# Attention rows kept in two tiles of four heads each, with stores of their own; gate weights loaded two steps earlier; the first q unit loaded from ScalarE's queue

## The chip, the cores and the metric

The kernel runs on one core of one Trainium2 chip. The metric is device time of one execution in microseconds, the median of several runs. The five instruction queues of the core that matter here are TensorE (PE, with its weight loads PEld), VectorE (DVE), ScalarE (ACT), GpSimd (POOL) and SyncE (SP); nearly all DMAs of this kernel are issued by SP, one after the other in the order of its queue.

## The reference

A linear attention feeds a mixture of experts. Cut to what matters:

```python
# q, k, v: (8 batches, 8 heads, 576 rows, 64), w_phi (64, 128), float32
def phi(x):
    p = einsum('bhsd,df->bhsf', x, w_phi)
    p = p - max(abs(p), axis=-1, keepdims=True)
    return concatenate([exp(p), exp(-p)], axis=-1)         # 256 features
kv  = einsum('bhsf,bhsd->bhfd', phi(k), v);  z = sum(phi(k), axis=2)
att = einsum('bhsf,bhfd->bhsd', phi(q), kv) / (einsum('bhsf,bhf->bhs', phi(q), z)[..., None] + 1e-6)
x   = att.transpose(0, 2, 1, 3).reshape(4608, 512)        # one row per token, 8 heads side by side
out = x.copy()
rows with x @ w_skip > 0 choose e = argmax(x @ w_gate), g = its softmax weight:
    out = x + g * (maximum(x @ w1[e], 0) @ w2[e])           # 8 experts, 512 -> 1024 -> 512
```

## The kernel before

The program has an attention part (to about 385 us) and an expert part after it.

**Units and steps.** The attention works on units of one batch and four heads: unit n is batch n // 2, heads 0 to 3 if n is even ("first half", `hq` 0) and 4 to 7 if odd ("second half", `hq` 1). There are 16 units for k and 16 for q, called k0 to k15 and q0 to q15 below. A loop over steps `t` takes half a unit (one pair of heads) of k and of q per step, q two steps behind k, so that unit n of k and unit n - 1 of q both enter at step 2n. In a step DVE transposes the loaded tile (`xT<-raw`, L316), PE projects it (`ps_A`, L327), DVE takes the maximum and subtracts it (L337, L338), ACT takes the exponentials (L352, L369), PE sums over k (`ps_K`, L408), ACT copies that to `kva` (L415), POOL copies a part of it to `kvs` (L420), PE turns that (`ps_V`, L360) and multiplies q (`ps_O`, L473), ACT copies the result to `os` (L477), and POOL divides it by its denominator into the row tile `xm` (L456) and the logits tile `lgm` (L458). The orders of PE, DVE, ACT and POOL are written out by hand from step 3 to step 35; SP's order is set by a scheduler, which puts a DMA where its own estimate has it ready.

**Loads.** `st_load` brings a unit of k or q with 8 DMAs of 32 x 18 x 32 elements (`raw<-in_k_dram`, `raw<-in_q_dram`, L283), `st_loadv` a unit of v with 4 larger ones (`v<-in_v_dram`, L292) and 4 small ones (`vt<-in_v_dram`, L299). There are four `raw` buffers, so k and q are loaded about one unit ahead. `setup_aug` loads the weights of the gate and of the skip score (`wgs`, L137 and L138), which POOL copies into `wgd` (L142) for the logits; it is called in step 3.

**Row tiles and stores.** Each batch has one tile `xm` of 128 x 4 x 514: 512 columns for eight heads, then the gate weight and the row's number. The last 64 rows of two batches share a tile `xt`. The first half's four heads are stored to `xrows` (a table in memory from which the experts gather their rows) when its two pairs are done: `store_half`, L493, and L495 for `xt`, columns 0 to 255. The second half's columns, with gate and number, follow later (`store_rows`, L591 and L593), and the function `rest` writes all 512 columns of a batch to the output (L671, 4 DMAs; L676, 4 for `xt` in odd batches). POOL writes the second half's heads into the same tile `xm` out of which the first half's store reads. Although these are other columns, the program makes the write wait for the store, as the order of POOL further down shows.

**Expert part.** After the counts of batch 5, `pick` chooses experts; SP loads weight chunks of 512 KB (`wraw_c<-in_moe_w_dram`, L188 and L191), ACT and POOL or DVE split them (L199, L204) and PE multiplies. The first experts' loads stand in SP's queue among the last stores of the attention.

Of the kernel before, what the change touches and what calls it, by code (L numbers as in the profile page):

```python
# [8 lines left out]
F32 = mybir.dt.float32  # L9
# [3 lines left out]
AF = mybir.ActivationFunctionType  # L13
# [4 lines left out]

P = 128
SLOT = 256  # L20
CFG = {'late': 1, 'gp': (0, 1, 2, 4, 6, 8, 9, 11, 12, 14, 17, 19, 21), 'rows': 9.0, 'tab': (2, 4, 5, 6, 6, 7, 8, 9, 10, 11, 12, 13, 16, 20, 32), 'ql': 0, 'cp': 0, 'seq': ('E', 'E', 'E', 'C', 'C', 'SC', 'C', 'DS', 'C', 'D'), 'post': (2, 4, 1), 'man': (3, 36), 'eng': ('PE', 'DVE', 'Activation', 'Pool'), 'nb': {'K': 1, 'O': 1, 'A': 2, 'P': 3, 'U': 2}, 'apools': (('ld', 2), ('hl', 4), ('up', 5), ('zp', 2), ('ep', 7), ('kvp', 5), ('ac', 1), ('xp', 3)), 'mpools': (('rawp', 1), ('mx', 2), ('wseta', 1), ('mo', 2), ('wsetb', 1), ('wsetc', 1), ('rawq', 1)), 'lag': (2, 2, 3, 0), 'order': ('Lv12KQebRcdBuExzwl', 'L01aKQ2ebRcdBuExwzy'), 'vl': 0, 'at': 3, 'eb': (2, 2), 'ub': 4, 'stage': (1, 1, 2, 2), 'dve': ('0', '1n', '2k', 'qt'), 'pd': 1}


@with_exitstack
def kernel(
# [20 lines left out]
    NQ = H // 4  # L46
# [8 lines left out]
    XW = DM + 2  # L55
# [19 lines left out]
    ac = pools["ac"]  # L75
# [155 lines left out]
    with actx:  # L231
# [26 lines left out]
        kva_of = {}  # L258
        kva_last = [None]
        xt_of = {}  # L260
        xm_of = {}
        et_of = {}
        kvt_of = {}
        kvs_of = {}
# [8 lines left out]
                c.pop(0)()  # L273
                last = c

        def st_load(u):
            src = kv_in[u.kind]
            u.raw = ld.tile([P, 2, 18, 32], F32, tag="raw", name="raw", bufs=4)
            for pr in range(2):
                for hd in range(2):  # L280
                    for dh in range(2):
                        r = (2 * hd + dh) * 32
                        nc.sync.dma_start(  # L283
                            out=u.raw[r:r + 32, pr],
                            in_=src[u.g, pr][hd * 32:hd * 32 + 32, :, dh * 32:dh * 32 + 32],
                        )

        def st_loadv(u):
            u.v0 = ld.tile([P, 4, 4 * D], F32, tag="v", name="v")
            u.vt = vts[u.g % len(vts)]  # L290
            for q4 in range(4):
                nc.sync.dma_start(  # L292
                    out=u.v0[q4 * 32:q4 * 32 + 32].rearrange("p h (t c) -> p h t c", c=D),
                    in_=vv[u.g][:, :, 4 * q4:4 * q4 + 4, :],
                )
            for pr in range(2):
                for q2 in range(2):
                    r = pr * 64 + q2 * 32
                    nc.sync.dma_start(out=u.vt[r:r + 32, pr, :, 0:D], in_=vv[u.g][:, 2 * pr:2 * pr + 2, 16 + q2, :])  # L299

        def st_v(u):
            u.v = vms[u.g % len(vms)]
# [159 lines left out]
        def st_use_q(u, pr, th):  # L462
            if th == 0:
                u.os = xp.tile([P, 8, NAUG], F32, tag="os", name="os", bufs=2)
            kva = kva_of[u.g]
            ov = bank("O")[:, 0:4 * NAUG].rearrange("p (t c) -> p t c", c=NAUG)
            e = u.e[pr]
            h0 = u.hq * 4 + 2 * pr
            for j in range(2):
                for hd in range(2):  # L470
                    for half in range(2):
                        for s in range(2):
                            nc.tensor.matmul(  # L473
                                ov[s * 64:s * 64 + 64, 2 * j + hd, :], e[:, half, s, 4 * hd + 2 * th + j],
                                kva[:, half, 2 * pr + hd, :], start=(half == 0), stop=(half == 1),
                            )
            nc.scalar.activation(out=u.os[:, 4 * th:4 * th + 4], in_=ov, func=AF.Copy)  # L477
            if th == 0:
                return
            if u.hq == 0 and pr == 0:  # L480
                xm_of[u.b] = (
                    xp.tile([P, 4, XW], F32, tag="xm", name="xm"),
                    xp.tile([P, 4, H, E + 1], F32, tag="lgm", name="lgm"),
                )
            xm, lgm = xm_of[u.b]

            def finish():
                c = slice(0, 4 * D)
                if pr == 0:
                    return  # L490
                if u.hq == 0:
                    def store_half(b=u.b, xm=xm):
                        nc.sync.dma_start(out=rowm[b][:, :, c], in_=xm[:, :, c])  # L493
                        if b % 2 == 1:
                            nc.sync.dma_start(out=rowt[b // 2][:, c], in_=xt_of[b // 2][0][:, 0, c])  # L495
                    later.append((now[0] + 1, store_half, "R"))
                else:
                    later.append((now[0] + CFG["pd"], lambda: post(u.b), "R"))

            norms.append(norm(u.os, 8, xm[:, :, h0 * D:(h0 + 2) * D].rearrange("p a (h d) -> p a h d", d=D),  # L500
                              lgm[:, :, h0:h0 + 2, :], 4) + [finish])

        def st_use_qt(u):

            if u.b % 2 == 0:
# [12 lines left out]
            nc.scalar.activation(out=os, in_=ov, func=AF.Copy)
            if u.hq == 0:
                xt_of[u.b // 2] = (  # L520
                    xp.tile([P, 1, XW], F32, tag="xt", name="xt"),
                    xp.tile([P, 1, H, E + 1], F32, tag="lgt", name="lgt"),
                )
            xt, lgt = xt_of[u.b // 2]
            norms.append(norm(os, 4, xt[:, :, u.hq * 4 * D:(u.hq + 1) * 4 * D].rearrange("p a (h d) -> p a h d", d=D),
                              lgt[:, :, u.hq * 4:(u.hq + 1) * 4, :], 1))

        def sm(tag, shape, dt=F32, bufs=2):
# [1 line left out]

        def post(b):
            last = b == B - 1
            xm, lgm = xm_of[b]
            t0 = 9 * (b // 2) + 4 * (b % 2)
            parts = [(xm, lgm, 0, 4)]
            if b % 2 == 1:
                xt, lgt = xt_of[b // 2]
                parts.append((xt, lgt, 4, 1))
            nt = 4 if b % 2 == 0 else 5
            T = slice(t0, t0 + nt)  # L540
# [42 lines left out]
            def gates():  # L583
                for xx, lg, o, n in parts:
                    nc.scalar.activation(
                        out=xx[:, :, DM + 1:XW], in_=sid[:, t0 + o:t0 + o + n].rearrange("p (t o) -> p t o", o=1), func=AF.Copy)
                    nc.vector.reciprocal(out=xx[:, :, DM:DM + 1], in_=gt[:, o:o + n].rearrange("p (t o) -> p t o", o=1))

            def store_rows():
                c = slice(4 * D, XW)  # L590
                nc.sync.dma_start(out=rowm[b][:, :, c], in_=xm[:, :, c])  # L591
                if b % 2 == 1:
                    nc.sync.dma_start(out=rowt[b // 2][:, c], in_=xt[:, 0, c])  # L593

            if last:
                best()
                exps()
                hot()
                gates()
                store_rows()  # L600
            else:
                best()
                for dt, f in zip(CFG["stage"], (exps, hot, gates, store_rows)):
                    later.append((now[0] + dt, f, "R"))
            S = 4
            nsh = S * E
# [59 lines left out]
                later.append((now[0], add, "R"))  # L666

            def rest():
                for q4 in range(4):
                    rr = slice(q4 * 32, q4 * 32 + 32)  # L670
                    nc.sync.dma_start(out=outv[b][:, q4 * 4:q4 * 4 + 4, :], in_=xm[rr, :, 0:DM])  # L671
                if b % 2 == 1:
                    for par in range(2):
                        for q2 in range(2):
                            rr = slice(par * 64 + q2 * 32, par * 64 + q2 * 32 + 32)
                            nc.sync.dma_start(out=outv[b - 1 + par][:, 16 + q2, :], in_=xt[rr, 0, 0:DM])  # L676

            if last:
                rests.extend((rank, rest))
# [45 lines left out]
        later = []  # L725
# [15 lines left out]
        for t in range(NPR + F + LQ + 2):  # L741
# [7 lines left out]
                setup_aug()  # L749

            if t == CFG["ql"]:
                st_load(units["q"][0])
            u = unit("k", t + CFG["vl"])
            if u:
                st_loadv(u)
# [626 lines left out]
```

## Time and profile before

| | us |
|---|---|
| median of 3 runs | 653.09 (650.76 to 654.57) |
| the profiled execution, its own time | 649.49 |
| its span, first to last instruction | 647.8 |
| PE busy in it | 542.2 (84%) |
| DVE busy | 445.8 (69%) |
| ACT busy | 340.3 (53%) |
| POOL busy | 304.4 (47%) |
| SP's queue moved by DMA | 97.61 MB, 58.1% of 16 DMA engines' span |

All later numbers are of the profiled execution, whose own time lies 1.7 us over its span and 3.6 us under the median of the runs. In the views, a row of the timeline gives start, duration, engine, line, operation, tiles, count, and in brackets the idle time before it with what ended it. A row of waits gives who waited for whom: total, times, longest. SP has no busy share in the page, since issuing a DMA is not counted as work; its rows in the timeline show how long each issue held the queue.

### The profile page before, as it was taken

The page shows a single profiled execution, that of the slowest core. Times are in us where ns is not written, and L with a number is a line of the kernel's source. Part 1 is how long each engine was busy: PE and PEld are TensorE (multiplying, and loading weights), DVE is VectorE, ACT ScalarE, POOL GpSimd, SP SyncE. Part 2 cuts the span into 40 slices and gives each one's busy share as a digit, 9 for nine tenths or more (in the row PEclk, how much of TensorE's full clock was granted, in tenths as well). Part 3 has the DMA queues.
Part 4 walks back from the last instruction along what each step waited for, and adds up shares of the span by engine and source line. Part 5 has one row for each costly group of instructions (what it writes and reads, how often), then busy time and mean ns, then how long its engine had stood idle before and what let it go on. Part 6 is the DMA issues. An engine that isn't in the chain of part 4 may idle for free. (4 is left out here: it accounts for less than half of the span.)

```text
span 647.8 us, 20883 instructions
## 1 busy us (share of the span) xinstructions
PE 542.2 (84%) x8638; PEld 502.0 (77%) x8638; DVE 445.8 (69%) x787; ACT 340.3 (53%) x561; POOL 304.4 (47%) x497
## 2 busy tenths in 40 slices
PE   2648977979969698798798679779999988999994
PEld 2648977879869698798797677659888978898893
DVE  5528865858947678478586376994887788856751
ACT  2136755645747367466665533433466755774630
POOL 2012314524434335234354974797466958469121
PEclk9869997989979989799899899798999999999998
DMA  6665567566675675766623768668758787687500
GB/s 111 113 106 118 97 126 151 111 169 126 111 202 111 131 171 106 199 109 129 149 76 79 260 185 288 210 220 253 231 180 269 239 296 251 232 278 261 199 18 28
DMA packets 223746, 108.47 MB, mean 167 GB/s; under 512 B 162339, under 2 KB 204451, under 8 KB 223650
## 3 DMA queue, kind: packets, MB, share of 16 engines
q1 hardware_dynamic: 220320, 97.61, 58.1%
q0 software_dynamic: 3200, 9.45, 4.2%
q8 instruction: 69, 1.13, 0.7%
q14 instruction: 27, 0.22, 0.1%
q10 hardware_dynamic: 130, 0.07, 0.0%
HBM read 83.86 MB, written 24.02 MB: 167 GB/s over the span
## 5 line engine op out<-in xcount | busy, mean ns | idle before, releaser
L204 POOL TENSOR_TENSOR w<-wraw_c,w 128x256 fp32r<-128x256 f32 x124 | 116.3, 970 | 38.3 <-ACT w L199 30.1
L337 DVE TENSOR_REDUCE m<-ps_A 128x8 f32<-128x1024 f32 x64 | 77.8, 1216 | 82.0 <-PE ps_A L327 82.0
L199 ACT ACTIVATE w<-wraw_c 128x1024 fp32r<-128x1024 f32 x96 | 98.1, 1051 | 23.0 <-DMA wraw_c<-in_moe_w_dram 18.7
L204 DVE TENSOR_TENSOR w<-wraw_c,w 128x1024 fp32r<-128x1024 f32 x65 | 85.4, 1325 | 18.5 <-ACT w L199 18.2
L456 POOL TENSOR_TENSOR xm<-os,rec 128x512 f32<-128x512 f32 x32 | 34.5, 1078 | 125.3 <-DMA xrows<-xm 66.6
L473 PE MATMUL ps_O<-kva,eq 128*64 128x74 f32 x2048 | 80.9, 232 | 6.0 <-ACT os L477 5.9
L408 PE MATMUL ps_K<-vm,ek 128*64 128x65 f32 x2048 | 79.3, 224 | 7.9 <-POOL vm L303 4.8
L327 PE MATMUL ps_A<-wsrc,xT 64*128 64x128 f32 x1024 | 82.2, 316 | 3.1 <-DVE ut L338 3.1
L408 PEld LDWEIGHTS ps_K<-vm,ek 128*64 128x64 f32 x2048 | 73.3, 140 | 9.5 <-POOL vm L303 5.0
L473 PEld LDWEIGHTS ps_O<-kva,eq 128*64 128x64 f32 x2048 | 72.7, 140 | 9.6 <-ACT os L477 6.2
L327 PEld LDWEIGHTS ps_A<-wsrc,xT 64*128 64x128 f32 x1024 | 75.9, 226 | 4.8 <-PE ps_V L360 4.7
L338 DVE TENSOR_TENSOR u<-ps_A,m 128x1024 f32<-128x1024 f32 x64 | 77.2, 1206 | 0.5
L369 ACT ACTIVATE eq<-ps_V 128x1024 f32<-128x1024 f32 x64 | 65.6, 1026 | 10.2 <-PE ps_V L360 9.9
L1006 PE MATMUL ps_O<-w,hh 128*128 128x512 f32 x160 | 65.2, 407 | 2.5 <-DVE o L953 2.5
L352 ACT ACTIVATE ek<-u 128x1024 f32<-128x1024 f32 x64 | 64.1, 1056 | 3.0 <-DVE u L338 3.0
L939 POOL DMA_INDIRECT out_dram<-o,si x22 | 29.1, 1324 | 53.5 <-DVE si L938 46.8
L1010 PE MATMUL ps_O<-w,hh 128*128 128x512 f32 x120 | 48.4, 403 | 3.4 <-POOL w L204 3.4
L477 ACT ACTIVATE os<-ps_O 128x296 f32<-128x296 f32 x64 | 26.8, 419 | 46.4 <-PE ps_O L473 45.3
L1011 PE MATMUL ps_O<-w,hlo 128*128 128x512 f32 x120 | 48.3, 403 | 0.0
L316 DVE STREAM_TRANSPOSE xT<-raw 128x512 f32<-128x512 f32 x64 | 44.4, 695 | 5.1 <-DMA raw<-in_k_dram 5.1
L360 PE MATMUL ps_V<-ident,kvs 64*128 64x64 f32 x128 | 10.5, 261 | 40.0 <-POOL kvs L420 40.0
L993 PE MATMUL ps_P<-x,w 128*128 128x256 f32 x144 | 37.9, 294 | 4.6 <-DVE x L870 4.6
(266 smaller groups left out, 1110.0 us busy)
## 6 DMA issues: line engine op xcount, KB each, us to landing
wraw_c<-in_moe_w_dram SPq DMA_DIRECT2D x96, 512.0 KB, 4.7
raw<-in_k_dram SPq DMA_DIRECT2D x128, 72.0 KB, 3.1
raw<-in_q_dram SPq DMA_DIRECT2D x128, 72.0 KB, 2.9
v<-in_v_dram SPq DMA_DIRECT2D x64, 128.0 KB, 3.0
out_dram<-xm SPq DMA_DIRECT2D x32, 256.0 KB, 4.3
xrows<-xm SPq DMA_DIRECT2D x8, 516.0 KB, 5.1
xrows<-xm SPq DMA_DIRECT2D x8, 512.0 KB, 4.4
vt<-in_v_dram SPq DMA_DIRECT2D x64, 16.0 KB, 2.6
```

What stands on the lines that cost most here:

```text
L199: nc.scalar.activation(out=hi, in_=raw, func=AF.Copy)
L204: eng.tensor_tensor(out=lo[:, r], in0=raw[:, r], in1=hi[:, r].bitcast(F32), op=ALU.subtract)
L327: nc.tensor.matmul(p[:, hd, j * NF:(j + 1) * NF], xT[r], wsrc[r], start=True, stop=True)
L337: lambda: nc.vector.tensor_reduce(out=m, in_=pv, axis=AX.X, op=ALU.max, apply_absolute_value=True),
L338: lambda: nc.vector.tensor_tensor(out=uu, in0=pv, in1=m.rearrange("p h (j o) -> p h j o", o=1).broadcast_to([P, 2, n, NF]), op=ALU.subtract),
L352: nc.scalar.activation(out=o, in_=uu, func=AF.Exp, scale=(1.0, -1.0)[a])
L369: return [lambda a=a: nc.scalar.activation(out=e[:, a].rearrange("p s g c -> p s (g c)"), in_=t, func=AF.Exp, scale=(1.0, -1.0)[a]) for a ...
L408: nc.tensor.matmul(o[s * 64:s * 64 + 64, hd, half, :], e[:, half, s * 64:s * 64 + 64], x, start=(g == 0), stop=(g == 4))
L473: nc.tensor.matmul(ov[s * 64:s * 64 + 64, 2 * j + hd, :], e[:, half, s, 4 * hd + 2 * th + j], kva[:, half, 2 * pr + hd, :], start=(half == ...
L1006: nc.tensor.matmul(y[sub], hh[:, t], wh[:, fi, :], start=first, stop=False)
L1010: nc.tensor.matmul(y[sub], hh[:, t], wl[:, fi, :], start=False, stop=False)
L1011: nc.tensor.matmul(y[sub], hlo[:, t], wh[:, fi, :], start=False, stop=last)
```

## The change

Three things change.

1. The row tile of a batch becomes two, one per four heads: `xm0` with 256 columns and `xm1` with 258, and `xt` likewise, each with three buffers. The table store of a half reads a whole tile. The output store is split as well: `store_out` is called once per half, with 4 DMAs of half the width each (and 4 for `xt` in odd batches); the first half's runs two steps after its last pair, no longer with the second half's.
2. `setup_aug` is called in step 1, not 3 (`'at'`); in the order of SP that is behind the second load of k.
3. The first unit of q is loaded with its 8 DMAs from ACT's queue (`'qq'`). (`'vq'` is 0 and changes nothing.)

```diff
-CFG = {... 'at': 3, ...}
+CFG = {... 'at': 1, ... 'vq': 0, 'qq': 1}
...
+        HW = (4 * D, XW - 4 * D)
...
-            if u.hq == 0 and pr == 0:
-                xm_of[u.b] = (
-                    xp.tile([P, 4, XW], F32, tag="xm", name="xm"),
...
+            if pr == 0:
+                xm_of[u.g] = xp.tile([P, 4, HW[u.hq]], F32, tag="xm%d" % u.hq, name="xm")
...
                 if u.hq == 0:
-                    def store_half(b=u.b, xm=xm):
-                        nc.sync.dma_start(out=rowm[b][:, :, c], in_=xm[:, :, c])
-                        if b % 2 == 1:
-                            nc.sync.dma_start(out=rowt[b // 2][:, c], in_=xt_of[b // 2][0][:, 0, c])
-                    later.append((now[0] + 1, store_half, "R"))
+                    later.append((now[0] + 1, lambda: store_rows(u.b, 0), "R"))
+                    later.append((now[0] + 2, lambda: store_out(u.b, 0), "R"))
...
+        def store_rows(b, hq):
+            c = slice(hq * 4 * D, hq * 4 * D + HW[hq])
+            nc.sync.dma_start(out=rowm[b][:, :, c], in_=xm_of[b * NQ + hq])
+            if b % 2 == 1:
+                nc.sync.dma_start(out=rowt[b // 2][:, c], in_=xt_of[b // 2, hq][:, 0])
+
+        def store_out(b, hq):
+            c = slice(hq * 4 * D, (hq + 1) * 4 * D)
+            for q4 in range(4):
+                rr = slice(q4 * 32, q4 * 32 + 32)
+                nc.sync.dma_start(out=outv[b][:, q4 * 4:q4 * 4 + 4, c], in_=xm_of[b * NQ + hq][rr, :, 0:4 * D])
+            if b % 2 == 1:
+                for par in range(2):
+                    for q2 in range(2):
+                        rr = slice(par * 64 + q2 * 32, par * 64 + q2 * 32 + 32)
+                        nc.sync.dma_start(out=outv[b - 1 + par][:, 16 + q2, c], in_=xt_of[b // 2, hq][rr, 0, 0:4 * D])
...
             def rest():
-                for q4 in range(4):
-                    rr = slice(q4 * 32, q4 * 32 + 32)
-                    nc.sync.dma_start(out=outv[b][:, q4 * 4:q4 * 4 + 4, :], in_=xm[rr, :, 0:DM])
...
+                store_out(b, 1)
...
-                st_load(units["q"][0])
+                st_load(units["q"][0], nc.scalar if CFG["qq"] else nc.sync)
```

What this does to the queues is seen at three places. The lines of the two kernels differ by a few; names and shapes are the same.

SP's queue at the start, before; `x8` counts DMAs:

```order
L283 DMA raw<-in_k_dram 32x18x32 x8
L283 DMA raw<-in_q_dram 32x18x32 x8
L292 DMA v<-in_v_dram 32x4x256 x4
L299 DMA vt_107<-in_v_dram 32x2x64 x4
L283 DMA raw<-in_k_dram 32x18x32 x8
L292 DMA v<-in_v_dram 32x4x256 x4
L299 DMA vt_108<-in_v_dram 32x2x64 x4
L283 DMA raw<-in_k_dram 32x18x32 x8
L283 DMA raw<-in_q_dram 32x18x32 x8
L137 DMA wgs<-in_moe_w_gate_dram 128x4x8
L138 DMA wgs<-in_moe_w_skip_dram 128x4x1
```

And now:

```order
L285 DMA raw<-in_k_dram 32x18x32 x8
L294 DMA v<-in_v_dram 32x4x256 x4
L301 DMA vt_107<-in_v_dram 32x2x64 x4
L285 DMA raw<-in_k_dram 32x18x32 x8
L137 DMA wgs<-in_moe_w_gate_dram 128x4x8
L138 DMA wgs<-in_moe_w_skip_dram 128x4x1
L294 DMA v<-in_v_dram 32x4x256 x4
L301 DMA vt_108<-in_v_dram 32x2x64 x4
L285 DMA raw<-in_k_dram 32x18x32 x8
L285 DMA raw<-in_q_dram 32x18x32 x8
```

The eight loads of q0 are gone from SP (they stand on ACT behind its first activation), and the gate weights stand behind k1 instead of q1.

SP's queue around the stores of the first two batches, before (from q4 to the stores of batch 1):

```order
L283 DMA raw<-in_q_dram 32x18x32 x8
L299 DMA vt_109<-in_v_dram 32x2x64 x2
L493 DMA xrows<-xm 512x1x256
L299 DMA vt_107<-in_v_dram 32x2x64 x2
L292 DMA v<-in_v_dram 32x4x256 x4
L671 DMA out_dram<-xm 32x4x512 x4
L283 DMA raw<-in_k_dram 32x18x32 x8
L283 DMA raw<-in_q_dram 32x18x32 x8
L299 DMA vt_107<-in_v_dram 32x2x64 x2
L495 DMA xrows<-xt 128x256
L299 DMA vt_108<-in_v_dram 32x2x64 x2
L292 DMA v<-in_v_dram 32x4x256 x4
```

The same stretch now:

```order
L511 DMA out_dram<-xm 32x4x256 x4
L285 DMA raw<-in_k_dram 32x18x32 x8
L285 DMA raw<-in_q_dram 32x18x32 x8
L301 DMA vt_109<-in_v_dram 32x2x64 x2
L301 DMA vt_107<-in_v_dram 32x2x64 x2
L294 DMA v<-in_v_dram 32x4x256 x4
L511 DMA out_dram<-xm 32x4x256 x4
L285 DMA raw<-in_k_dram 32x18x32 x8
L285 DMA raw<-in_q_dram 32x18x32 x8
L301 DMA vt_107<-in_v_dram 32x2x64 x2
L505 DMA xrows<-xt 128x256
L516 DMA out_dram<-xt 32x256 x4
```

The first half's stores (`xrows<-xm` stands in the row ahead of these, too) have moved in front of k5 and q4; the output of a batch takes two groups of four DMAs instead of one, and that of `xt` likewise.

POOL's queue where it writes the second half of batch 0, with what each instruction waits for (`DMAHW` is a DMA's semaphore), before:

```order
L420 COPY kvs<-kva 128x2x128 [waits Activation_49,Pool_49]
L448 TENSOR_SCALAR den<-os 128x8 [waits Activation_49]
L303 COPY vm_105<-v 128x16x64 [waits DMAHW6_49,DMAHW5_49,DMAHW7_49,DMAHW0_49,PE_49]
L456 TENSOR_TENSOR xm<-os,rec 128x4x128 [waits DMAHW3_49,DVE_49]
L458 TENSOR_TENSOR lgm<-os,rec 128x4x18
L448 TENSOR_SCALAR den<-os 128x8 [waits Activation_49]
L420 COPY kvs<-kva 128x2x128 [waits Activation_49]
```

And now:

```order
L422 COPY kvs<-kva 128x2x128 [waits Activation_49,Pool_49]
L450 TENSOR_SCALAR den<-os 128x8 [waits Activation_49]
L305 COPY vm_105<-v 128x16x64 [waits DMAHW6_49,DMAHW5_49,DMAHW7_49,DMAHW0_49,PE_49]
L458 TENSOR_TENSOR xm<-os,rec 128x4x128 [waits DVE_49]
L460 TENSOR_TENSOR lgm<-os,rec 128x4x18
L450 TENSOR_SCALAR den<-os 128x8 [waits Activation_49]
L422 COPY kvs<-kva 128x2x128 [waits Activation_49]
```

The order stays; the write into `xm` no longer waits for a DMA. Of the 32 such writes 13 waited for a DMA before, and 3 do now (writes into a tile whose buffer had been stored three batches earlier).

More of the change, by code (lines that the diff above doesn't have):

```diff
@@ L20 @@
 SLOT = 256
-CFG = {'late': 1, 'gp': (0, 1, 2, 4, 6, 8, 9, 11, 12, 14, 17, 19, 21), 'rows': 9.0, 'tab': (2, 4, 5, 6, 6, 7, 8, 9, 10, 11, 12, 13, 16, 20, 32), 'ql': 0, 'cp': 0, 'seq': ('E', 'E', 'E', 'C', 'C', 'SC', 'C', 'DS', 'C', 'D'), 'post': (2, 4, 1), 'man': (3, 36), 'eng': ('PE', 'DVE', 'Activation', 'Pool'), 'nb': {'K': 1, 'O': 1, 'A': 2, 'P': 3, 'U': 2}, 'apools': (('ld', 2), ('hl', 4), ('up', 5), ('zp', 2), ('ep', 7), ('kvp', 5), ('ac', 1), ('xp', 3)), 'mpools': (('rawp', 1), ('mx', 2), ('wseta', 1), ('mo', 2), ('wsetb', 1), ('wsetc', 1), ('rawq', 1)), 'lag': (2, 2, 3, 0), 'order': ('Lv12KQebRcdBuExzwl', 'L01aKQ2ebRcdBuExwzy'), 'vl': 0, 'at': 3, 'eb': (2, 2), 'ub': 4, 'stage': (1, 1, 2, 2), 'dve': ('0', '1n', '2k', 'qt'), 'pd': 1}
+CFG = {'late': 1, 'gp': (0, 1, 2, 4, 6, 8, 9, 11, 12, 14, 17, 19, 21), 'rows': 9.0, 'tab': (2, 4, 5, 6, 6, 7, 8, 9, 10, 11, 12, 13, 16, 20, 32), 'ql': 0, 'cp': 0, 'seq': ('E', 'E', 'E', 'C', 'C', 'SC', 'C', 'DS', 'C', 'D'), 'post': (2, 4, 1), 'man': (3, 36), 'eng': ('PE', 'DVE', 'Activation', 'Pool'), 'nb': {'K': 1, 'O': 1, 'A': 2, 'P': 3, 'U': 2}, 'apools': (('ld', 2), ('hl', 4), ('up', 5), ('zp', 2), ('ep', 7), ('kvp', 5), ('ac', 1), ('xp', 3)), 'mpools': (('rawp', 1), ('mx', 2), ('wseta', 1), ('mo', 2), ('wsetb', 1), ('wsetc', 1), ('rawq', 1)), 'lag': (2, 2, 3, 0), 'order': ('Lv12KQebRcdBuExzwl', 'L01aKQ2ebRcdBuExwzy'), 'vl': 0, 'at': 1, 'eb': (2, 2), 'ub': 4, 'stage': (1, 1, 2, 2), 'dve': ('0', '1n', '2k', 'qt'), 'pd': 1, 'vq': 0, 'qq': 1}
 @with_exitstack
@@ L260 @@
         xt_of = {}
-        xm_of = {}
+        xm_of, lg_of, lgt_of = {}, {}, {}
+        HW = (4 * D, XW - 4 * D)
         et_of = {}
@@ L274, in run, with st_load @@
                 last = c
-        def st_load(u):
+        def st_load(u, eng=None):
+            eng = eng or nc.sync
             src = kv_in[u.kind]
@@ L282, in st_load @@
                         r = (2 * hd + dh) * 32
-                        nc.sync.dma_start(
+                        eng.dma_start(
                             out=u.raw[r:r + 32, pr],
@@ L298, in st_loadv @@
                     r = pr * 64 + q2 * 32
-                    nc.sync.dma_start(out=u.vt[r:r + 32, pr, :, 0:D], in_=vv[u.g][:, 2 * pr:2 * pr + 2, 16 + q2, :])
+                    (nc.scalar if CFG["vq"] else nc.sync).dma_start(out=u.vt[r:r + 32, pr, :, 0:D], in_=vv[u.g][:, 2 * pr:2 * pr + 2, 16 + q2, :])
         def st_v(u):
@@ L479, in st_use_q @@
                 return
-            if u.hq == 0 and pr == 0:
-                xm_of[u.b] = (
-                    xp.tile([P, 4, XW], F32, tag="xm", name="xm"),
-                    xp.tile([P, 4, H, E + 1], F32, tag="lgm", name="lgm"),
-                )
-            xm, lgm = xm_of[u.b]
+            if pr == 0:
+                xm_of[u.g] = xp.tile([P, 4, HW[u.hq]], F32, tag="xm%d" % u.hq, name="xm")
+                if u.hq == 0:
+                    lg_of[u.b] = xp.tile([P, 4, H, E + 1], F32, tag="lgm", name="lgm")
+            xm, lgm = xm_of[u.g], lg_of[u.b]
             def finish():
-                c = slice(0, 4 * D)
                 if pr == 0:
@@ L491, in finish @@
                 if u.hq == 0:
-                    def store_half(b=u.b, xm=xm):
-                        nc.sync.dma_start(out=rowm[b][:, :, c], in_=xm[:, :, c])
-                        if b % 2 == 1:
-                            nc.sync.dma_start(out=rowt[b // 2][:, c], in_=xt_of[b // 2][0][:, 0, c])
-                    later.append((now[0] + 1, store_half, "R"))
+                    later.append((now[0] + 1, lambda: store_rows(u.b, 0), "R"))
+                    later.append((now[0] + 2, lambda: store_out(u.b, 0), "R"))
                 else:
                     later.append((now[0] + CFG["pd"], lambda: post(u.b), "R"))
-            norms.append(norm(u.os, 8, xm[:, :, h0 * D:(h0 + 2) * D].rearrange("p a (h d) -> p a h d", d=D),
+            norms.append(norm(u.os, 8, xm[:, :, pr * 2 * D:(pr + 1) * 2 * D].rearrange("p a (h d) -> p a h d", d=D),
                               lgm[:, :, h0:h0 + 2, :], 4) + [finish])
+        def store_rows(b, hq):
[13 more added lines that the diff above has]
+                        nc.sync.dma_start(out=outv[b - 1 + par][:, 16 + q2, c], in_=xt_of[b // 2, hq][rr, 0, 0:4 * D])
         def st_use_qt(u):
@@ L518, in st_use_qt @@
             nc.scalar.activation(out=os, in_=ov, func=AF.Copy)
+            xt_of[u.b // 2, u.hq] = xp.tile([P, 1, HW[u.hq]], F32, tag="xt%d" % u.hq, name="xt")
             if u.hq == 0:
[L520 to L525, printed above, removed]
+                lgt_of[u.b // 2] = xp.tile([P, 1, H, E + 1], F32, tag="lgt", name="lgt")
+            xt, lgt = xt_of[u.b // 2, u.hq], lgt_of[u.b // 2]
+            norms.append(norm(os, 4, xt[:, :, 0:4 * D].rearrange("p a (h d) -> p a h d", d=D),
                               lgt[:, :, u.hq * 4:(u.hq + 1) * 4, :], 1))
@@ L532, in post @@
             last = b == B - 1
-            xm, lgm = xm_of[b]
+            xm, lgm = xm_of[b * NQ + 1], lg_of[b]
             t0 = 9 * (b // 2) + 4 * (b % 2)
@@ L536, in post @@
             if b % 2 == 1:
-                xt, lgt = xt_of[b // 2]
+                xt, lgt = xt_of[b // 2, 1], lgt_of[b // 2]
                 parts.append((xt, lgt, 4, 1))
@@ L585, in gates @@
                     nc.scalar.activation(
[L586 to L593, printed above, removed]
+                        out=xx[:, :, HW[1] - 1:HW[1]], in_=sid[:, t0 + o:t0 + o + n].rearrange("p (t o) -> p t o", o=1), func=AF.Copy)
+                    nc.vector.reciprocal(out=xx[:, :, HW[1] - 2:HW[1] - 1], in_=gt[:, o:o + n].rearrange("p (t o) -> p t o", o=1))
             if last:
@@ L599, in post @@
                 gates()
-                store_rows()
+                store_rows(b, 1)
             else:
                 best()
-                for dt, f in zip(CFG["stage"], (exps, hot, gates, store_rows)):
+                for dt, f in zip(CFG["stage"], (exps, hot, gates, lambda: store_rows(b, 1))):
                     later.append((now[0] + dt, f, "R"))
@@ L668, in rest @@
             def rest():
-                for q4 in range(4):
-                    rr = slice(q4 * 32, q4 * 32 + 32)
[L671 to L676, printed above, removed]
+                store_out(b, 1)
             if last:
```

## The prediction

> **What bounds the kernel now.** I read the waits of the whole run first, then POOL's and SP's timelines around the longest of them, then SP's from start to end. Totals, times and longest:
>
> ```profile
> POOL xm L456 <- DMA xrows<-xm: 66.6, 7, 13.0
> ...
> PE ps_V L360 <- POOL kvs L420: 40.0, 9, 10.6
> ...
> POOL wgd L142 <- DMA wgs<-in_moe_w_skip_dram: 16.9, 1, 16.9
> ...
> DVE xT L316 <- DMA raw<-in_k_dram: 5.1, 2, 4.4
> ```
>
> POOL stands still seven times until a table store has landed, and behind it in its queue waits the copy `kvs`, for which PE waits 40.0 us in all. One of the seven, in POOL's and SP's timelines:
>
> ```profile
> 98.81 1.04 POOL L456 TENSOR_TENSOR xm<-os,rec 128x512 f32<-128x512 f32 x1 [13.03 <-DMA xrows<-xm]
> ...
> 100.51 0.40 POOL L420 COPY kvs<-kva 128x256 f32<-128x256 f32 x1
> ```
>
> ```profile
> 87.40 5.62 SPq L283 DMA_DIRECT2D raw<-in_q_dram  x8
> 93.12 1.03 SPq L299 DMA_DIRECT2D vt<-in_v_dram  x2
> 94.26 0.59 SPq L493 DMA_DIRECT2D xrows<-xm  x1
> 94.95 1.54 SPq L299 DMA_DIRECT2D vt<-in_v_dram  x2
> 96.58 1.80 SPq L292 DMA_DIRECT2D v<-in_v_dram  x4
> 99.89 2.87 SPq L671 DMA_DIRECT2D out_dram<-xm  x4
> 102.85 6.43 SPq L283 DMA_DIRECT2D raw<-in_k_dram  x8
> ```
>
> The store of 94.26 was late because SP was issuing loads without a pause. That is the real bound: SP's queue goes like this from the first load to the last one of q15:
>
> ```profile
> 0.80 6.04 SPq L283 DMA_DIRECT2D raw<-in_k_dram  x8
> 6.89 5.35 SPq L283 DMA_DIRECT2D raw<-in_q_dram  x8
> ...
> 297.41 5.88 SPq L283 DMA_DIRECT2D raw<-in_q_dram  x8
> ...
> 310.00 3.12 SPq L671 DMA_DIRECT2D out_dram<-xm  x4
> 313.22 6.49 SPq L283 DMA_DIRECT2D raw<-in_q_dram  x8
> 333.85 0.56 SPq L493 DMA_DIRECT2D xrows<-xm  x1
> ```
>
> An issue holds SP some 0.4 to 0.6 us plus 0.05 to the next. From 0.80 to 319.71 I find one pause over 1 us, ahead of 99.89, where the v loads had ended at 98.38. Compute is slower than that queue only by the false wait; without it, it would run ahead until it waits for `raw`. So I count what SP's queue gets shorter and longer, not the 40.0 us.
>
> **Where the loads meet compute.** DVE at the end of the attention (k15, q14, then q15), and the median from issue to landing:
>
> ```profile
> 317.89 0.70 DVE L316 STREAM_TRANSPOSE xT<-raw 128x512 f32<-128x512 f32 x1
> ...
> 319.62 0.69 DVE L316 STREAM_TRANSPOSE xT<-raw 128x512 f32<-128x512 f32 x1
> ...
> 337.47 0.70 DVE L316 STREAM_TRANSPOSE xT<-raw 128x512 f32<-128x512 f32 x1
> ```
>
> ```profile
> raw<-in_q_dram SPq DMA_DIRECT2D x128, 72.0 KB, 2.9
> ```
>
> q14 was issued until 303.29 (297.41 + 5.88), landed at 306.2 and was read at 319.62: 13.4 us early. This lead is all that compute can win, less what SP's queue grows up to q14. The two steps from 317.89 to 337.47 stay: q15, issued until 319.71, has landed 15 us before 337.47, so q14 decides.
>
> **The parts and their cost on SP up to q14.**
>
> *q0 to ACT:* eight issues gone, -5.4 (5.35 and one gap). ACT idles 7.50 us at the start, which hides them there:
>
> ```profile
> 10.97 0.72 ACT L352 ACTIVATE ekt<-ut 128x256 f32<-128x256 f32 x2 [7.50 <-DVE ut L338]
> ```
>
> Here a rule of the Trainium skill can be weighed. "DMA: Bandwidth & Descriptors", section "Issuing engines are not separate DMA queues", says that issuing from several engines saves only the sequencer's issue time, which is usually small beside the transfer. By that this part is worth nothing and the sum is 5.4 us less good; the trace agrees on what is saved, but not on small, since here SP's issues fill 319 us.
>
> *The false wait:* the store now precedes k5, POOL does not wait for it, and SP's own pause before 99.89 (1.5 us, it waited for POOL's `xm`) goes: -1.5.
>
> *Stores of `xm` in two groups.* Groups of four at full width, and the nearest rows for half width: four v loads move the same 128 KB in runs of the same 1 KB, and `vt` and `xt` bound the small ones (min/median/max ns):
>
> ```profile
> 143.26 3.36 SPq L671 DMA_DIRECT2D out_dram<-xm  x4
> ...
> 185.09 2.88 SPq L671 DMA_DIRECT2D out_dram<-xm  x4
> ...
> 228.84 3.51 SPq L671 DMA_DIRECT2D out_dram<-xm  x4
> ...
> 269.87 3.31 SPq L671 DMA_DIRECT2D out_dram<-xm  x4
> ```
>
> ```profile
> 12.28 2.04 SPq L292 DMA_DIRECT2D v<-in_v_dram  x4
> 14.44 1.77 SPq L299 DMA_DIRECT2D vt<-in_v_dram  x4
> ...
> 118.85 2.76 SPq L292 DMA_DIRECT2D v<-in_v_dram  x4
> ...
> 135.64 3.30 SPq L676 DMA_DIRECT2D out_dram<-xt  x4
> ...
> 222.07 2.46 SPq L676 DMA_DIRECT2D out_dram<-xt  x4
> ```
>
> ```profile
> L292 SPq DMA_DIRECT2D v<-in_v_dram x64: 312/430/1814, 12.3 to 290.7; - x64
> L299 SPq DMA_DIRECT2D vt<-in_v_dram x64: 363/428/1859, 14.4 to 304.0; - x64
> ```
>
> Before q14 stand five full `xm` groups (2.87, 3.36, 2.88, 3.51, 3.31; 15.9 us) and then eleven half ones: two each of batches 0 to 4 and the first of batch 5. At 2.05 each, between 1.80 and 2.76 and near the first v group, that is 22.55: +6.65. Of `xt`, two full groups (5.8) become five half ones; at 2.45, the shorter of the two full ones and above the 1.77 of `vt`: 12.25, +6.45. The table store of batch 5 moves ahead of q14: +0.6. Medians of 430 and 428 ns for 128 KB and 16 KB say that an issue's price does not fall with its size; only the occasional long ones do.
>
> Sum: -5.4 - 1.5 + 6.65 + 6.45 + 0.6 = +6.8. q14 has landed at 306.2 + 6.8 = 313.0 and is read there, 6.6 us before 319.62. Bounds: if every half group takes 1.77, the sum is 16 x 1.77 - 21.7 + 0.6 - 6.9 = +0.3 and the gain 13.1; if each costs what a full one does (3.2 and 2.9), it is 35.2 + 14.5 - 28.0 = +21.7, and the loss 8.3.
>
> *Gate weights two steps earlier:* two issues change places, no cost on SP. POOL's 16.9 us wait and PE's longest, 10.6 us on `kvs` behind it, end sooner. I count 0: it only brings compute forward at the start, onto the same queue of loads; bounds 0 and, if compute set the pace, 10.6.
>
> **Into the experts.** POOL waits once more for the table store, SP waits for POOL's last `xm`, and the second expert's weights wait behind SP's stores:
>
> ```profile
> 382.34 2.06 POOL L456 TENSOR_TENSOR xm<-os,rec 128x512 f32<-128x512 f32 x1 [3.94 <-DMA xrows<-xm]
> ```
>
> ```profile
> 384.43 0.36 SPq L671 DMA_DIRECT2D out_dram<-xm  x1
> ...
> 393.41 2.31 SPq L188 DMA_DIRECT2D wraw_c<-in_moe_w_dram  x4
> ```
>
> ```profile
> 396.89 1.06 ACT L199 ACTIVATE w<-wraw_c 128x1024 fp32r<-128x1024 f32 x1 [11.40 <-DMA wraw_c<-in_moe_w_dram]
> ```
>
> ```profile
> 420.00:440.00 20.00, 15.40 (x72) 13.21 (x71) 19.49 (x19) 6.40 (x8) 19.34 (x16) 0.84 0.63 211
> ```
>
> POOL's 3.94 us go; ten small stores follow SP's wait in both kernels, so its loads and ACT's split come 3.9 us sooner: -3.9. Bounds: 0, if the stretch to 440 (DVE 19.49 and POOL 19.34 busy of 20) is full anyway; 8, if the ten issues also shrink to 0.48 each (4.8 us instead of the 9.0 from 384.43 to 393.41).
>
> **Sum.** 6.6 + 3.9 = 10.5 us less: 649.5 - 10.5 = 639.0 for the profiled execution. That execution was 3.6 us under the median of the runs, so as a median 653.1 - 10.5 = 642.6, say 643.
>
> **Rivals.**
>
> - *The split stores outweigh everything.* Mechanism: an output issue costs SP what a full one costs, whatever its width; SP's queue to q14 grows by 21.7, q14 is read at 327.9, and with 3.9 back the time is 653.1 + 8.3 - 3.9 = 657.5. It decides from a half group of 2.8 us on: 16 x 2.83 - 28.0 = 17.3, which is the lead of 13.4 and the 3.9 together. For it: the equal medians, and a full `xt` issue of 64 KB dearer than the v one. Against: the v groups, same in bytes and runs, at 1.8 to 2.8. The rule against it in the Trainium skill, "DMA: Bandwidth & Descriptors", "Rules for kernel authors": many small transfers should become one large, since under 64 KB one pays mostly overhead. The halved `xt` stores go from 64 to 32 KB, so by that rule the 8.7 above is the right term for `xt`, and the gain is 2.2 less. The medians agree with it.
> - *SP is not the bound.* If its long issues are waits in disguise that faster compute shortens, PE's 40.0 us on `kvs` go: 653.1 - 40.0 = 613. Against: eight k loads took 6.04 us at the very start, when nothing had to be waited for.
> - *Nothing moves.* The stall of POOL turns into one of DVE on `raw`, SP's queue grows by about 13 to q14, and the experts' stretch to 440 absorbs the 3.9: 653, within 3.3 us (0.5%, what a measurement of this kernel can tell from no change).
>
> **Chances.** Forecast (SP's queue sets the end, 3.3 to 20 us gained) 0.63; nothing 0.18; split stores outweigh 0.14; SP not the bound 0.05. Faster by over 0.5% holds the first and the last: 0.68; same 0.18; slower 0.14. The bounds give 653.1 - 13.1 - 8 = 632 and 653.1 + 8.3 = 661; I round the one to 633 and cut the other at 656, which leaves out the worst half of the split stores' case and the case of 613.
>
> **What would show it.** Right: POOL's seven waits for `xrows<-xm` and PE's for `kvs` nearly gone; in their place DVE waiting for `raw`, 20 us or more in all; SP still without pauses, with q15 issued until about 325; half groups at 2 us; POOL's wait for `wgs` gone; q14's transposes near 313. Wrong: half groups near 3 us; SP pausing for POOL's rows or for free buffers; or DVE never waiting for `raw`, by which SP would not have been the bound.

## The result

| | before | changed |
|---|---|---|
| first set, median of 20 runs each | 653.83 us (650.31 to 657.78) | 651.18 us (644.14 to 655.10) |
| second set, median of 23 and 12 runs | 651.55 us | 652.39 us (647.25 to 654.86) |
| ratio, first set | | 0.9943, interval 0.9916 to 0.9970 |
| ratio, second set | | 1.0014, interval 0.9989 to 1.0039 |
| profiled execution | 649.49 us | 652.22 us |

The forecast was 643. By the medians the first set gives a gain of 2.7 us, the second none, and the two intervals leave anything from a gain of 0.8% to a loss of 0.4%. The ratios leave out runs in a slower state of the chip, three of the changed kernel's 20 among them, so they are not the quotients of the medians. The profile shows the stall that the change was to remove gone, with another in its place.

### The profile page after: what moved, and what is told of

The parts are those of the page before. It is cut to its first block, busy times and chain, and to the rows that moved or that the text cites. A ratio compares the mean times of both kernels' runs of the same rounds, so it can differ in the third digit from the quotient of the medians.

```text
span 650.5 us, 20923 instructions
## 1 busy us (share of the span) xinstructions
PE 547.9 (84%) x8638; PEld 507.0 (78%) x8638; DVE 453.9 (70%) x787; ACT 338.8 (52%) x561; POOL 297.3 (46%) x497
## 5 line engine op out<-in xcount | busy, mean ns | idle before, releaser
L204 POOL TENSOR_TENSOR w<-wraw_c,w 128x256 fp32r<-128x256 f32 x124 | 110.5, 923 | 35.6 <-ACT w L199 25.1
L204 DVE TENSOR_TENSOR w<-wraw_c,w 128x1024 fp32r<-128x1024 f32 x65 | 84.0, 1302 | 20.2 <-ACT w L199 19.7
L329 PE MATMUL ps_A<-wsrc,xT 64*128 64x128 f32 x1024 | 83.9, 320 | 0.9 <-DVE ut L340 0.9
L329 PEld LDWEIGHTS ps_A<-wsrc,xT 64*128 64x128 f32 x1024 | 78.2, 232 | 1.5 <-PE ps_V L362 1.3
L329 PE MATMUL ps_A<-wsrc,xTt 64*128 64x128 f32 x128 | 18.4, 384 | 47.7 <-DVE xTt L318 35.6
L318 DVE STREAM_TRANSPOSE xT<-raw 128x512 f32<-128x512 f32 x64 | 44.6, 698 | 13.3 <-DMA raw<-in_q_dram 8.5
L329 PEld LDWEIGHTS ps_A<-wsrc,xTt 64*128 64x128 f32 x128 | 11.9, 231 | 51.3 <-DVE xTt L318 49.6
```

The lines of the kernel that those rows point to most:

```text
L204: eng.tensor_tensor(out=lo[:, r], in0=raw[:, r], in1=hi[:, r].bitcast(F32), op=ALU.subtract)
L329: nc.tensor.matmul(p[:, hd, j * NF:(j + 1) * NF], xT[r], wsrc[r], start=True, stop=True)
```

## The profile after

Waits of the changed kernel (who waited for whom: total, times, longest):

```profile
DVE xTt L318 <- DMA raw<-in_q_dram: 21.7, 11, 3.2
DVE xT L318 <- DMA raw<-in_q_dram: 8.5, 7, 3.0
POOL wgd L142 <- DMA wgs<-in_moe_w_skip_dram: 7.4, 1, 7.4
PE ps_V L362 <- POOL kvs L422: 2.0, 3, 0.7
```

POOL's 66.6 us for `xrows<-xm` have no row any more, and PE's 40.0 us for `kvs` are 2.0. DVE now waits 30.2 us for loads of q, where before it had waited for loads of k alone. SP's queue shows why; its rows at the start, around the first stores and at the end of the attention:

```profile
0.80 7.73 SPq L285 DMA_DIRECT2D raw<-in_k_dram  x8
...
13.88 5.29 SPq L285 DMA_DIRECT2D raw<-in_k_dram  x8
...
79.11 0.59 SPq L503 DMA_DIRECT2D xrows<-xm  x1
79.74 3.52 SPq L511 DMA_DIRECT2D out_dram<-xm  x4
83.36 7.19 SPq L285 DMA_DIRECT2D raw<-in_k_dram  x8
...
100.60 1.83 SPq L511 DMA_DIRECT2D out_dram<-xm  x4
...
311.87 5.80 SPq L285 DMA_DIRECT2D raw<-in_q_dram  x8
...
321.96 2.80 SPq L511 DMA_DIRECT2D out_dram<-xm  x4
324.87 5.94 SPq L285 DMA_DIRECT2D raw<-in_q_dram  x8
```

q14 is issued until 317.67 (311.87 + 5.80); before it was 303.29. SP's queue up to there has grown by 14.4 us, and the lead that q14 had was 13.4. DVE at the same place (the first row is k15, the second and third q14):

```profile
314.71 0.70 DVE L318 STREAM_TRANSPOSE xT<-raw 128x512 f32<-128x512 f32 x1
317.05 0.71 DVE L318 STREAM_TRANSPOSE xT<-raw 128x512 f32<-128x512 f32 x1 [0.53 <-DMA raw<-in_q_dram]
...
320.28 0.31 DVE L318 STREAM_TRANSPOSE xTt<-raw 128x128 f32<-128x128 f32 x1 [2.32 <-DMA raw<-in_q_dram]
```

The transposition that stood at 319.62 stands at 317.05, but the small one behind it waits for a load of q14 until 320.28. Step by step, the n-th transposition of `xT` in both timelines: the changed kernel is 12.3 us ahead at 48 us (the gate weights came earlier), 14.2 ahead at 108, 9.2 at 235 and nothing at 304. Compute ran ahead and the loads caught up with it.

## The experiments

Each is compared with the kernel before, run beside it on the same chip. In the diffs `-` is the kernel that it is made from.

**No output stores.** From the changed kernel.

```diff
         def store_out(b, hq):
+            return
```

> The changed kernel without the DMAs that write the attention rows to the output (`store_out` issues nothing), so the plain copy of the rows is left out of the output. Theory (SP's queue sets the pace of the attention, and the doubled output stores ate the lead): the 64 stores up to q14 cost SP 32.0 + 10.7 us, so q14 is issued until about 275 instead of 317.7, DVE's 30 us of waits for `raw` are gone, and the time falls by 20 to 30 us, to 621 to 631. Rival (compute has its own limit just under the old pace, and the stores only fill idle time of SP): q14 is issued earlier but the steps of the attention stay where they are, 646 to 651.

Measured: 614.25 us, ratio 0.9392 (0.9329 to 0.9455). SP at q14 and q15:

```profile
277.37 6.20 SPq L285 DMA_DIRECT2D raw<-in_q_dram  x8
...
286.41 5.77 SPq L285 DMA_DIRECT2D raw<-in_q_dram  x8
```

q14 is issued until 283.57, 34.1 us earlier, the last transposition of the attention stands 34.9 us earlier, and the whole kernel is 37 us faster than the changed one. The steps of the attention follow SP's queue nearly one for one, so the stores' time on that queue is what set the pace. The gain is above the theory's 20 to 30, which I had taken from DVE's waits alone; q14 came 9 us later than expected, since the loads of k and v were charged 8 us more when the stores were gone (time from the end of one issue to the end of the next, summed). Nor are DVE's waits gone, as the theory had it:

```profile
DVE xTt L318 <- DMA raw<-in_q_dram: 9.7, 7, 2.7
DVE xT L318 <- DMA raw<-in_q_dram: 4.4, 2, 2.3
```

So DVE still runs into the loads here. The granted clock of TensorE is higher too, 1.00 from 100 to 300 us against 0.92 and 0.90 in the changed kernel; what that adds to the gain was not separated.

**One table store per batch.** From the kernel before: one row tile, no first-half table store.

```diff
                 if u.hq == 0:
-                    def store_half(b=u.b, xm=xm):
-                        ...
-                    later.append((now[0] + 1, store_half, "R"))
+                    pass
...
             def store_rows():
-                c = slice(4 * D, XW)
+                c = slice(0, XW)
```

> The kernel before with the false wait taken away in another way: one row tile as before, but no table store of the first half; one table store of all 514 columns stands where that of the second half stood. POOL then writes the second half with no store in flight, and SP issues fewer DMAs than before, not more. Theory (SP's queue): SP's queue to q14 is shorter by its pause of 1.5 us and by six table stores of `xm` and three of `xt`, some 5 us, so q14 lands near 299.5 and the lead of 13.4 can be used in full and 6 more: 630 to 640. If compute meets a limit of its own on the way, less of it: 640 to 645. Rival (the lost lead of the changed kernel has nothing to do with the number of stores; whoever removes the false wait finds DVE or PE at its own limit): 649 to 654, as the changed kernel.

Measured: 638.97 us, ratio 0.9808 (0.9728 to 0.9887). The false wait is gone, SP has fewer issues instead of more, and 14 us are won. q14 is issued until 297.80:

```profile
291.97 5.83 SPq L283 DMA_DIRECT2D raw<-in_q_dram  x8
```

DVE is 16.1 us ahead of before at 318 us and 9.4 at the end of the attention. The difference was lost to a stop of ACT ahead of its copy of the row numbers into `xm`:

```profile
297.77 2.01 ACT L352 ACTIVATE ek<-u 128x1024 f32<-128x1024 f32 x2
306.29 0.21 ACT L581 ACTIVATE xm<-sid 128x4 f32<-128x4 f32 x1 [6.50 <-issue]
306.40 1.01 ACT L369 ACTIVATE eq<-ps_V 128x1024 f32<-128x1024 f32 x1
```

In the program's order that copy belongs to a later batch, whose tile takes the buffer of one three batches earlier, and it waits for the stores out of that buffer. The trace agrees: ACT's wait for semaphores ends at 306.17, and the table store that SP issued at 301.73 has landed at 306.14. A kernel without that wait was not tried.

**The same with both parts at the start.** q0 from ACT's queue and gate weights in step 1, as in the change.

> The kernel with one table store per batch (one full row tile, no table store of the first half; 639.0 in its run) together with the two parts at the start of the change. Theory (SP's queue): 2 us less to q14, 635.5 to 638. Rival (that kernel's pace is no longer SP's but compute's, and its first steps hang on the gate weights): the 12 us at the start come through at least in part, 627 to 634. Rival 2: nothing, 638 to 640.

Measured: 637.61 us, ratio 0.9764 (0.9720 to 0.9808). This beats the kernel before by 15.6 us in its own set, and stands 13.6 to 14.8 below the two medians of the changed kernel. The 12 us of lead at the start do not come through here either: DVE's waits for loads of q rise from 7.6 to 19.9 us.

**Only the start, only the split.** The first is the kernel before with `'at': 1` and q0 on ACT; the second the changed kernel with `'at': 3, 'qq': 0`.

> The kernel before with only the two parts at the start: q0's eight loads issued from ACT's queue, gate weights in step 1. Row tiles and stores as before, so POOL's false wait stays. Theory (SP's queue sets the pace, and q0 on ACT shortened it in the changed kernel by about 2.4 us, not by 5.4): each table store that POOL waits for stands about 2 us earlier in SP's queue, 650 to 652.5 beside 653.8. As the prediction had it: 5.4 us less, 648. Rival (the 12 us by which DVE is ahead at 48 us of the changed kernel, through the earlier gate weights, are kept): 641 to 645.

> The changed kernel without the two parts at the start: q0 from SP's queue again, gate weights in step 3. Row tiles and stores split as in the change. Theory: no false wait, but SP's queue 2 us longer to q14 than in the changed kernel, so q14 is issued until about 320 and read near 323 instead of 319.6 before: 652 to 656, no gain over the kernel before. Rival (the split is what brought the 2.7 us, the start nothing): 650 to 652.

Measured: the start alone 651.42 us, ratio 0.9972 (0.9948 to 0.9997); the split alone 653.23 us, ratio 1.0012 (0.9988 to 1.0036). So the split of tiles and stores, the largest part of the change, brought nothing, and what the first set gained is about what the start brings. In the start's run POOL still waits for table stores,

```profile
POOL xm L457 <- DMA xrows<-xm: 78.4, 7, 20.0
```

and the longest of these waits takes the lead away: DVE is 13.3 us ahead at 48 us and 1.7 at 108. In the split's run q14 is issued until 318.93, as expected.

**Price by the issue or by bytes.** From the changed kernel, each half store in 8 DMAs of 16 partitions.

```diff
             for q4 in range(4):
-                rr = slice(q4 * 32, q4 * 32 + 32)
-                nc.sync.dma_start(out=outv[b][:, q4 * 4:q4 * 4 + 4, c], in_=xm_of[b * NQ + hq][rr, :, 0:4 * D])
+                for o in (0, 16):
+                    rr = slice(q4 * 32 + o, q4 * 32 + o + 16)
+                    nc.sync.dma_start(
+                        out=outv[b][o:o + 16, q4 * 4:q4 * 4 + 4, c], in_=xm_of[b * NQ + hq][rr, :, 0:4 * D])
```

> The changed kernel with each half output store of `xm` in 8 DMAs of 16 partitions (64 KB) instead of 4 of 32 (128 KB): same bytes, twice the issues. If an issue of a store costs SP what it did at double size (price by the issue): 44 more issues up to q14 at 0.6 to 0.73 us, q14 26 to 32 us later, 675 to 690. If it costs by bytes: the group of eight takes 2.9 us like that of four, 650 to 653. Between: 0.45 us each, as `vt` and `v` cost at the median, 668 to 675.

Measured: 670.87 us, ratio 1.0243 (1.0187 to 1.0298).

```profile
80.16 4.40 SPq L512 DMA_DIRECT2D out_dram<-xm  x8
103.08 4.77 SPq L512 DMA_DIRECT2D out_dram<-xm  x8
...
334.24 5.58 SPq L285 DMA_DIRECT2D raw<-in_q_dram  x8
```

The eleven groups up to q14 take 4.89 us in the mean instead of 2.84, and q14 is issued until 339.81, 22 us later. An issue of 128 KB was charged 0.73 us, one of 64 KB 0.62 (time from the end of one issue to the end of the next): half the bytes save a seventh. So it is nearly a price by the issue: the 44 issues more cost 0.50 us each on the way to q14, between the first expectation's 0.6 to 0.73 and the middle one's 0.45, and the time fell into the middle one's range. Since the bytes are the same, it is the number of issues that makes the queue longer.

**Output store ahead of the table store.** From the changed kernel.

```diff
-                    later.append((now[0] + 1, lambda: store_rows(u.b, 0), "R"))
-                    later.append((now[0] + 2, lambda: store_out(u.b, 0), "R"))
+                    later.append((now[0] + 1, lambda: store_out(u.b, 0), "R"))
+                    later.append((now[0] + 2, lambda: store_rows(u.b, 0), "R"))
```

> The changed kernel with the first half's output store issued one step earlier and its table store one step later, so that in SP's queue the four half stores stand ahead of the table store instead of right behind it. Same DMAs. In the changed kernel the half groups right behind a table store of 512 KB took 3.12 us in the mean, the others 2.50. Theory 1 (the table store ahead makes the stores behind it dear): the first halves' groups fall to 2.5 us or less, nothing else gets dearer, q14 is issued some 3.5 us earlier, 647 to 649. Theory 2 (the table store costs SP that time whoever stands behind it): the long issues move to the k loads behind it, 650 to 652. Theory 3 (a half group costs what its own bytes cost wherever it stands): groups stay near 2.9, 650 to 652, and the k loads behind it are unchanged.

Measured: 646.92 us, ratio 0.9937 (0.9903 to 0.9971), beside 652.39 of the changed kernel in the same set: 5.5 us less with the same DMAs.

```profile
79.66 1.82 SPq L511 DMA_DIRECT2D out_dram<-xm  x4
81.52 0.59 SPq L503 DMA_DIRECT2D xrows<-xm  x1
82.21 6.77 SPq L285 DMA_DIRECT2D raw<-in_k_dram  x8
...
99.78 1.87 SPq L511 DMA_DIRECT2D out_dram<-xm  x4
...
305.57 6.16 SPq L285 DMA_DIRECT2D raw<-in_q_dram  x8
```

The first of these groups took 3.52 us behind the table store and takes 1.82 ahead of it; the eleven average 2.20 us. Charged on SP up to q14, `xm`'s output stores fall from 31.2 (the changed kernel in the same set) to 25.3 us, 5.9 less, while the loads of k, q and v rise by 1.1, 1.0 and 3.0 and the other kinds fall by some 2.5. q14 is issued until 311.73 instead of 314.86, and the span is 4.0 us shorter. So the place right behind 512 KB does make the stores dear, as theory 1 had it, but "nothing else gets dearer" was wrong: of the 5.9 us the queue keeps 3.1.

**The queue of ACT instead of SP's.** From the changed kernel: the output stores (`store_out`) on `nc.scalar`; then the 64 `vt` loads (`'vq': 1`); then the fastest kernel with `vt` on ACT and all loads of v a unit earlier (`'vl': 2`, and v of unit 0 in step 0).

> The changed kernel with the same output stores issued from ACT's queue instead of SP's. Same DMAs, same bytes, another queue. Theory (what the half stores cost is SP's time for issuing them): SP's queue to q14 is shorter by about 42 us, as without these stores, and the time falls to 621 to 635, a few us above that of the kernel without stores, since ACT holds 80 issues of 0.5 to 0.7 us each. Rival 1 (the stores cost what they move: the writes delay the loads in the DMA engines, whoever issues them): the loads land as late as in the changed kernel, 648 to 653. Rival 2 (ACT waits in its order for POOL's rows and the exponentials come late): slower than 651.

> The changed kernel with the 64 small loads `vt` issued from ACT's queue instead of SP's; nothing else differs. Theory (SP's queue): SP loses about 37 us up to q14, ACT gains some 32 us of issuing beside 339 us of work; q14 is issued near 281, DVE no longer waits for `raw`, 621 to 635. Rival 1 (SP is not the pace): 649 to 653. Rival 2 (ACT's issues delay its exponentials, for which PE waits): SP's queue gets shorter as in the theory, but the time stays at 645 to 655 or above.

> The kernel with one table store per batch and both parts at the start (637.6 in its run), with the 64 small loads `vt` on ACT's queue and all loads of v a unit earlier. With `vt` on ACT in time for the same unit the changed kernel took 738.9, ACT stopping 7 to 15 us at each group of four. Theory 1 (ACT stopped because an issue of ACT waits for semaphores that SP's newest loads hold, not because the data were late): the stops stay, 700 to 740. Theory 2 (the loads were needed at once, so that ACT and PE waited for data): with a unit of lead the stops go, SP's queue is 35 us shorter, 610 to 630.

Measured: 666.53 us, ratio 1.0191 (1.0116 to 1.0265); 738.86, ratio 1.1316 (1.1245 to 1.1387); 727.74, ratio 1.1160 (1.1104 to 1.1216). All three are slower, and SP's queue did not get shorter as the theory had it: q14 is issued until 306.27 in the first, 11 us earlier instead of 42, and until 377.28 and 369.59 in the others, 60 and 52 us later than in the changed kernel. With `vt` on ACT SP stops itself, ahead of its loads of v, until POOL has copied the v before:

```profile
SPq L294 <- POOL vm L305: 83.6, 12, 10.8
```

ACT in the same run:

```profile
143.65 0.42 ACT L533 ACTIVATE ost<-ps_O 128x296 f32<-128x296 f32 x1 [0.70 <-PE ps_O L528]
151.52 2.78 ACTq L301 DMA_DIRECT2D vt<-in_v_dram  x4
154.35 0.60 ACT L387 ACTIVATE kvt<-ps_V 128x512 f32<-128x512 f32 x1 [10.28 <-DMA vt<-in_v_dram]
```

ACT stops from 144.1 to 151.5 before its first issue. What that group waits for in the program's order:

```
L533 ACTIVATE ost<-ps_O 128x296 [waits PE_49,Activation_49]
L301 DMA vt_107<-in_v_dram 32x2x64 [waits DMAHW6_49]
L301 DMA vt_107<-in_v_dram 32x2x64 [waits DMAHW7_49]
L301 DMA vt_107<-in_v_dram 32x2x64 [waits DMAHW0_49]
L301 DMA vt_107<-in_v_dram 32x2x64 [waits DMAHW1_49]
```

The eight semaphores `DMAHW0` to `DMAHW7` go round over the DMAs of both queues in program order, so ACT's issue waits until the DMA that had the semaphore last, one of SP's, has landed. The trace shows it stop by stop: ACT stands still for 6.0 to 8.7 us ahead of twelve groups of `vt`, and each time its issue starts 0.02 us after a landing on the semaphore that it waits for and then uses itself. In all twelve that semaphore had last been given to a load of q, which SP had issued 2.4 to 2.9 us before. Loading a unit earlier did not help (ACT still waits 99.9 us in all at `vt`): it was not the data that were late. With the output stores on ACT (96 issues, not the 80 expected) only one stop is as long as these, 12.0 us before 94.26; how the rest of its 15 us divides was not followed.

**The changed kernel once more.**

> The changed kernel once more, unaltered. In its first profile two groups of DVE instructions behind 394.87 and at 407.14 took 2.0 and 6.0 us longer than before while POOL split weights, which is as much as the steps into the experts had been ahead. Theory 1 (such a hold falls as DVE and POOL happen to meet in that execution): another profile shows the 72-element product at 0.2 to 0.8 us, and the span is 3 to 6 us shorter, 644 to 648. Theory 2 (the new order brings it every time): 6 us again and a span of 650.

Measured: 652.39 us, ratio 1.0014; the profiled execution has a span of 645.5 us. The long instruction of the first profile, and POOL beside it:

```profile
407.14 6.21 DVE L1119 TENSOR_TENSOR tm<-OH,pks 128x72 f32<-128x72 bf16 x1
```

```profile
407.64 5.63 POOL L204 TENSOR_TENSOR w<-wraw_c,w 128x256 fp32r<-128x256 f32 x8
```

and in the second profile:

```profile
407.13 0.77 DVE L1119 TENSOR_TENSOR tm<-OH,pks 128x72 f32<-128x72 bf16 x1
```

The span is 5 us shorter without it, inside the first theory's range, but half of that is not the hold's: the last transposition of the attention, ahead of it, already stands at 340.8 instead of 343.3. The median is not shorter, so this hold explains a part of the difference between two profiled executions and nothing of the verdict.

## Why the prediction was wrong

*What bounds the kernel: right.* SP's queue is the bound of the attention once the false wait is gone. Leaving out the output stores gave 37 us, leaving out the first half's table stores 14, doubling the issues of `xm`'s output cost 20.

*The false wait turns into one of DVE on `raw`: right.* 30.2 us, forecast 20 or more. The rival that SP is not the bound (613) fell; that number came only when the stores were taken away.

*Stores of `xm`, +6.65: the step that failed.* I priced a half group at 2.05 us, from v loads that follow other loads. It measured 2.84 in the mean: 3.12 for the six right behind a table store of 512 KB, 2.50 for the rest. The groups went from 15.9 to 31.2 us, +15.3; charged on SP up to q14, with the pause of 1.5 us in the 18.0 before, from 18.0 to 32.0, +14.0 (+13.2 in the second profile). With the output store ahead of the table store, the eleven groups took 2.20, near the 2.05. The changed order put a table store ahead of every first half's group, and I took no row for that place, though the two full `xt` groups that I show, 3.30 and 2.46, stand behind such a store.

The groups hide a second part of the error, which the traces show issue by issue. Up to q14, ten profiles (all but the three with more on ACT's queue) have 52 to 61 issues of 0.9 us or more, 68 to 81 us in all, whether SP makes 383 issues, as without output stores, or 491, as with eight to a group. From before to the change these long ones went from 58 to 54 (74.3 to 71.4 us) and all the others from 200.9 to 214.7 us, +13.8, nearly the whole growth. So the long issues in the five full groups (six of 1.0 us or more, 8.1 us of the 15.9) were not saved by taking those groups away; others in the queue were long instead. What makes an issue long, the runs do not show.

*`xt`, +6.45:* measured +4.7, from 6.0 to 10.7 charged. The price of 2.45 was too high: 2.07.

*q0 to ACT, -5.4:* measured -2.4 at k1, which is issued from 13.88 instead of 16.25 us. k0's eight issues got longer, 7.73 us instead of 6.04, and gaps appeared, because ACT's loads take turns at the same eight semaphores: the fifth load of k0 is issued at 5.64 instead of 3.78, when the load that ACT had issued first on its semaphore has landed (5.62). Calling the part hidden on ACT left out what it does to SP. Further on it is not these semaphores that hold SP: from 20 us to q14 no gap between two issues of the changed kernel is over 0.45 us.

*The sum:* +6.8 forecast, +14.4 measured (+11.6 in the second profile), against a lead of 13.4. Charged, that is +14.0 and +4.7 for the stores to the output, +1.4 for the table stores, -1.8 for q, +1.1 for k, and -5.0 for v and `vt`, which no term of the forecast had; without that luck q14 would have come later still. q14 was read from 317.1 to 320.3 instead of at 313.0: the gain of 6.6 was at most 2.6, and none at the last read. q15 was issued until 330.8, not 325.

*Gate weights, 0: right.* POOL's wait shrank from 16.9 to 7.4 us rather than vanishing, DVE got 12 us ahead, and the loads took it back.

*Into the experts, -3.9:* the second expert's loads came 6.3 us earlier,

```profile
387.13 6.92 SPq L188 DMA_DIRECT2D wraw_c<-in_moe_w_dram  x4
```

but in the first profile DVE took 8 us longer between 395 and 413 in two groups of instructions beside POOL; in the second, without the longer of these holds, the experts end 2.3 us ahead, hardly more than the attention with 2.1. It ended at its lower bound.

What came true is the third rival, "nothing moves", by the mechanism that it named: SP's queue longer by about 13, and the 3.9 absorbed. It had 0.18. "Split stores outweigh" named 2.83 us per half group as the point where the sign turns; the sixteen groups measured 2.60 in the mean (2.84 for `xm`, 2.07 for `xt`), a little under it. "Half groups near 3 us" was also the forecast's first sign of being wrong. The rule of the Trainium skill that spoke against the change ("DMA: Bandwidth & Descriptors", "Rules for kernel authors": many small transfers into one) deserved more weight: the trace agrees, with 0.71 us held for half the bytes against 0.80 for the whole, and 0.52 for 32 KB of `xt` against 0.72 for 64 KB.

## What to carry to other kernels

When one queue issues without a pause, count its issues before anything else: here the removal of a 66.6 us wait paid for itself only when it also removed issues (637.6 us), and paid nothing when it doubled the issues of the output. Take the price of an issue from the same place in the queue, not from the same size elsewhere, and do not count occasional long issues as saved with the groups that they stood in. And do not move issues to a compute engine's queue because that engine has idle time: it waits in order, and twelve stops of 6.0 to 8.7 us before its groups of issues went with a loss of 87 us.

## What the runs showed of the hardware

A group of four 128 KB stores took 1.82 us to issue at one place and 3.52 (3.18 in a second profile) right behind a 512 KB store, in two kernels that differ only in the order of the two. Why SP holds longer there, the runs do not show.

DVE's product of two SBUF tiles, 0.23 us before, took 6.21 us and ended (413.35) with the last of eight back-to-back POOL instructions (413.27). The Trainium skill, "SBUF — State Buffer", section "Who interferes with whom", says that a DVE instruction with two SBUF inputs contends with a GpSimd one that reads SBUF, and that the ports which the two share are an exclusive lock. The trace agrees on the blocking, and shows it here over eight instructions in a row, though DVE's row starts 0.50 us before the first of them. In the second profile the same product took 0.77 us, inside a series of the same eight.
